# Decay attention and an MLP on one core: v's load in two column halves, with the splits and the next maximum at other heads

## The chip, the cores and the metric

The kernel runs on one core of one Trainium2 chip. The metric is the device time of one execution in microseconds; lower is better. Beside the times there is one profiled execution, whose span (first to last instruction) is a little shorter than the time that is measured from outside.

## The reference

There are 8 batches of 8 heads, 576 rows and 64 columns a head. Attention comes first, then an MLP over all 4608 rows of 512 columns, with 2048 columns in its middle:

```python
scores = scale * np.matmul(q, k.transpose(0, 1, 3, 2))
log_f = np.log(np.clip(f, 0.0001, 1.0))
cum = np.cumsum(log_f, axis=-1)
scores = np.where(causal, -1000000000.0, scores + cum[:, :, :, None] - cum[:, :, None, :])
attn = np.exp(scores - np.max(scores, axis=-1, keepdims=True))
attn = attn / (np.sum(attn, axis=-1, keepdims=True) + 1e-09)
x = np.matmul(attn, v)              # then (B*S, H*D)
h = x @ w_in
g = h * np.clip(h + 3.0, 0.0, 6.0) / 6.0
return g @ w_out
```

## The kernel before

Every large product runs on TensorE (PE) in fp16, with each operand split into a high and a low part, and three matmuls for one product (high by high, high by low, low by high). To split v, the kernel first needs a power-of-two scale for each batch, and for that the largest absolute value of the batch's v.

The main loop goes over 68 units: four "A" units and eight "B" units for batch 0, which is cut differently, and 56 "F" units, one for each head of batches 1 to 7. The names in the listings carry the unit's number: unit 12 is head 0 of batch 1, unit 20 head 0 of batch 2, and so on, so unit 36 is head 0 of batch 4 and unit 40 is head 4 of batch 4. One F unit does this:

- SP loads q and k of the head into one of three buffers ST (L411), decay rows into TK and TQ (L417, L419), and copies the rounded parts within the chip into T7 and T1 (L453, L454, both called T in the profile). POOL rounds q and k (L446, L447) and makes the rests (L455, L458).
- PE makes the scores pn (L608, L611) in two halves of the head's rows, called pn_40_0 and pn_40_1 for unit 40. DVE adds the mask and takes row maxima (L619), and makes the bias nb (L625). ACT takes the exponential (L631) and casts it into a ring buffer (L645). DVE or POOL puts the rest beside it (L648, L654, L659).
- SP transposes the ring buffer into pT by DMA (L666), once for each half.
- PE multiplies pT with the split v into pav (L691 to L696). DVE divides by the row sums (L720 to L726). For every pair of heads, the result is split (xhl, L731, L732) and transposed by DMA into xT (L752).

Between the pieces of this, the MLP is filled in, in nine tiles of 512 rows. Its first product (L778 to L780) makes ph; ACT and DVE make r and the two parts of gT out of it (L788, L791, L792, L793). Its second product (L800 to L802) makes po from all of gT, which ACT scales and SP stores (L811, L812). With half a unit or so of shift, one batch of attention goes with one tile of the MLP, so the first product, the second product, and the next first product lie in turn beside the heads of a batch.

For v there is one buffer, vst, which holds a whole batch: 128 partitions, 5 chunks of rows, 8 heads of 65 columns (64 and one spare). The first 64 rows go into chunk 0 twice (L359, two DMAs); the rest, 4 chunks of 520 columns in fp32, comes in one DMA of 1040 KB (L360). `load_v` for the next batch stands at head 6 of a batch. `v_scale` for the next batch stands at head 7: two reductions on DVE, of three and of two chunks (L365), two small steps (L370, L371), a matmul with ones that spreads the maximum (L183), and four small steps that make the scale (L178 to L199). `v_split` makes the fp16 parts of one pair of heads in v16, which has three slots: two ACT and two DVE instructions (L396, L397). It stands at heads 1, 3 and 5 for pairs 1 to 3 of the batch, and at head 7 for pair 0 of the next batch.

The framework's scheduler sets the order of the instructions on each engine from this program. A statement's place gives it its rank; an instruction that is ready by the scheduler's reckoning may be put far ahead of its place. Each engine then takes its instructions strictly in that order, and so does SP with its DMAs. An instruction that waits therefore holds up all that stands behind it on its engine.

Of the kernel before, what the change touches and what calls it, by code (L numbers as in the profile page):

```python
# [15 lines left out]
ALU = mybir.AluOpType  # L16
AX = mybir.AxisListType
# [3 lines left out]
def kernel(  # L21
# [10 lines left out]
    nc = tc.nc  # L32

    NHEAD, D, S = qk.shape
# [72 lines left out]
    POOL_REST = ((0, 0, 0, 0), (0, 0, 0, 0))  # L107
    PIN_V = 1
    TQ = [cpool.tile([97, SP], F32R, name=f"TQ{i}") for i in range(NQK)]
    TK = [cpool.tile([97, SP], F32R, name=f"TK{i}") for i in range(NQK)]  # L110
# [31 lines left out]
    v0 = [t.rearrange("p (c e) -> p c e", e=VR) for t in v0]  # L142

    def v_parts(b):
        return v0 if b == 0 else [vst[:, 0:3], vst[:, 3:]]

    def v_chunk(b, c):
        return v_parts(b)[c // 3][:, c % 3]

# [198 lines left out]

    def load_v(b):
        src = vS[b]  # L350
        lo, hi = v_parts(b)
        with pinned() if PIN_V else nullcontext():
            if b == 0:
                nc.sync.dma_start(lo, src[0:3 * P].rearrange("(c p) e -> p c e", p=P))
                nc.sync.dma_start(hi[:, 0], src[3 * P:4 * P])
                nc.sync.dma_start(hi[:64, 1], src[4 * P:S])
            else:
                for p in (0, 64):
                    nc.sync.dma_start(vst[p:p + 64, 0], src[0:64])  # L359
                nc.sync.dma_start(vst[:, 1:], src[64:].rearrange("(c p) e -> p c e", p=P))  # L360

    def v_scale(b):
        pm = p2.tile([P, 2], F32, tag="pm", name=f"vm{b}")
        for i, t in enumerate(v_parts(b)):
            nc.vector.tensor_reduce(  # L365
                pm[:, i:i + 1], t.rearrange("p c (h e) -> p (c h) e", e=D + 1)[:, :, 0:D],
                axis=AX.XY, op=ALU.max, apply_absolute_value=True,
            )
            yield
# [554 lines left out]
    for i, (kind, n) in enumerate(VH):  # L924
# [7 lines left out]
        if ahead:  # L932
            load_c(i + 2)
        if b + 1 < B and h == 6:
            load_v(b + 1)
        if b and h % 2 == 1 and h < H - 1:
            v_split((n + 1) // 2)
        if moved is not None:
# [10 lines left out]
        fill(1)  # L949
        if b + 1 < B and h == 7:  # L950
            vq = v_scale(b + 1)
# [20 lines left out]
        fill(1)  # L972
        if b + 1 < B and h == 7:
            for _ in vq:
                pass
            if b:
                v_split((n + 1) // 2)
        for _ in range(wn - wn // 2):
# [59 lines left out]
```

## Time and profile before

| | |
|---|---|
| three runs | 1094.02, 1103.02, 1099.4 us |
| their median | 1099.4 us |
| span of the profiled execution | 1093.0 us |
| TensorE busy | 1013.8 us (93%) |
| VectorE, ScalarE, GpSimd busy | 728.9, 609.7 and 414.4 us |
| mean granted TensorE clock | 0.981 |
| data moved by DMA | 133.74 MB |

Only a span is known of the profiled execution; it is about 1 us under the fastest run. The table's busy times are sums over the whole span. How much of a stage TensorE uses, and who stops it there, has to be read from short stretches, from the waits, and from the chain of waits that ended last. In a row of the waits stand the total in microseconds, how many there were, and the longest. In a row of a timeline stand the start, the length, the engine, the line, the operation, the tile written and the tile read, and in square brackets the idle time ahead of it and what ended that. "SPq" marks the issue of a DMA on SP; its transfer goes on after it.

### The profile page before, as it was taken

Reading aid. Unit: us, or ns where it says so; the run is one execution under the profiler, and the core shown is the slowest. Engines: PE = TensorE matmul, PEld = TensorE weight load, DVE = VectorE, ACT = ScalarE, POOL = GpSimd, SP = SyncE. Lnnn points to the kernel's source line nnn. Section 1 sums busy time; section 2 is a strip of 40 time slices with the busy share of each in tenths; the row PEclk is TensorE's granted clock in tenths of the full one; section 3 lists DMA queues with packets and bytes.
Section 4 is the critical chain, followed back from the end, with each engine's and each line's share of the span. In section 5 each row is a group of like instructions: output and inputs, shape, how many; then the busy total and the mean of one; then the engine's idle time right before and its main releaser. Section 6 shows DMA issues by size and latency. Waiting matters only on the chain.

```text
span 1093.0 us, 20322 instructions
## 1 busy us (share of the span) xinstructions
PE 1013.8 (93%) x7074; PEld 576.3 (53%) x7074; DVE 728.9 (67%) x1903; ACT 609.7 (56%) x1285; POOL 414.4 (38%) x505
## 2 busy tenths in 40 slices
PE   2799977899999989998999889999999999999998
PEld 2568844755555545554555445555555554444443
DVE  7888889877887669756876588569856840520520
ACT  4786656756765557545754566458646831621520
POOL 8443465345545434444534335453555300000000
PEclk9999989999999989998999989999999999999999
DMA  8966447866767656566566755785566530000001
GB/s 251 283 196 211 119 101 131 182 139 137 169 136 155 144 138 130 108 145 155 108 121 129 170 105 116 146 185 104 116 136 145 98 77 29 1 5 34 1 1 39
DMA packets 261651, 133.74 MB, mean 122 GB/s; under 512 B 229445, under 2 KB 231037, under 8 KB 261549
## 3 DMA queue, kind: packets, MB, share of 16 engines
q1 hardware_dynamic: 261548, 132.45, 54.0%
q8 instruction: 56, 0.92, 0.4%
q14 instruction: 47, 0.38, 0.1%
HBM read 47.93 MB, written 9.73 MB: 53 GB/s over the span
## 4 chain that ended last, share of the span: by engine, by line
PE 59%; DMA 6%; DVE 4%; issue 3%; SPq 3%; ACT 3%; POOL 2%; POOLq 0%; DVEq 0%; ACTq 0%
PE po L800 9%; PE po L802 9%; PE po L801 9%; PE ph L778 8%; PE ph L779 8%; PE ph L780 8%; DMA pT<-ring 3%; PE pn L611 3%; PE pn L608 3%; DMA vst<-in_vS_dram 2%; SPq L752 2%; DVE pp L619 1%; ACT pp L631 1%; PE pav L695 1%; PE pav L696 1%
## 5 line engine op out<-in xcount | busy, mean ns | idle before, releaser
L778 PE MATMUL ph<-xT,w 128*128 128x512 f16 (+1 forms) x640 | 229.2, 364 | 19.6 <-DVE r L791 19.4
L779 PE MATMUL ph<-xT,w 128*128 128x512 f16 (+1 forms) x640 | 228.5, 363 | 0.0
L780 PE MATMUL ph<-xT,w 128*128 128x512 f16 (+1 forms) x640 | 228.2, 362 | 0.0
L801 PE MATMUL po<-w,gT 128*128 128x512 f16 x576 | 214.3, 381 | 7.3 <-DVE w L294 7.3
L800 PE MATMUL po<-w,gT 128*128 128x512 f16 x576 | 212.1, 381 | 3.0 <-ACT w L283 2.2
L802 PE MATMUL po<-w,gT 128*128 128x512 f16 x576 | 214.1, 381 | 0.0
L631 ACT ACTIVATE pp<-pp,nb 128x192 f32<-128x192 f32 x280 | 138.8, 553 | 128.2 <-DVE nb L625 127.9
L648 DVE TENSOR_TENSOR ring<-pp,ring 128x128 f16<-128x128 f32 (+2 forms) x216 | 135.0, 635 | 70.1 <-ACT ring L645 69.2
L791 DVE SCALAR_TENSOR_TENSOR r<-r,ph 128x512 f32<-128x512 f32 (+1 forms) x160 | 99.9, 626 | 104.6 <-ACT r L788 104.4
L788 ACT ACTIVATE r<-ph,bias_r,SC 128x256 f32<-128x256 f32 (+7 forms) x272 | 144.1, 571 | 37.2 <-PE ph L780 33.3
L458 POOL TENSOR_TENSOR T<-ST,T 64x576 fp32r<-64x576 f32 (+1 forms) x68 | 100.6, 1480 | 153.5 <-DMA T<-TK 149.6
L792 ACT CAST gT<-r 128x512 f16<-128x512 f32 (+1 forms) x160 | 91.9, 575 | 89.6 <-DVE r L791 89.5
L619 DVE CUSTOM_DVE_ANT_0 pp<-pn,W 128x192 f32<-128x192 f32 x280 | 123.3, 482 | 26.1 <-PE pn L611 19.8
L608 PE MATMUL pn<-TK,TQ 68*128 68x192 f32 x336 | 127.0, 390 | 5.6 <-issue 4.0
L793 DVE TENSOR_TENSOR gT<-r,gT 128x512 f16<-128x512 f32 (+1 forms) x160 | 110.4, 693 | 29.2 <-ACT gT L792 28.5
L611 PE MATMUL pn<-T,T 128*128 128x192 f32 x336 | 116.2, 375 | 0.4 <-POOL T L458 0.4
L645 ACT CAST ring<-pp 128x192 f16<-128x192 f32 x280 | 115.7, 452 | 0.0
L455 POOL TENSOR_TENSOR T<-ST,TQ 64x576 fp32r<-64x576 f32 (+2 forms) x68 | 96.8, 1423 | 18.4 <-PE pn L611 8.7
L779 PEld LDWEIGHTS <-w 128*128 128x128 f16 x640 | 63.1, 99 | 75.2 <-issue 26.2
L780 PEld LDWEIGHTS <-w 128*128 128x128 f16 x640 | 63.2, 99 | 65.8 <-issue 9.2
L802 PEld LDWEIGHTS <-gT 128*128 128x128 f16 x576 | 56.5, 98 | 76.0 <-issue 14.6
L778 PEld LDWEIGHTS <-w 128*128 128x128 f16 x640 | 62.4, 99 | 59.1 <-issue 10.8
(136 smaller groups left out, 1713.6 us busy)
## 6 DMA issues: line engine op xcount, KB each, us to landing
ST<-in_qk_dram SPq DMA_DIRECT2D x64, 288.0 KB
T<-TK SPq DMA_DIRECT2D x64, 144.0 KB
out_dram<-o SPq DMA_DIRECT2D x36, 256.0 KB
ring<-in_w_out_dram SPq DMA_DIRECT2D x16, 512.0 KB
T<-TQ SPq DMA_DIRECT2D x56, 144.0 KB
vst<-in_vS_dram SPq DMA_DIRECT2D x7, 1040.0 KB
ring<-in_w_in_dram SPq DMA_DIRECT2D x9, 512.0 KB
w<-in_w_in_dram SPq DMA_DIRECT2D x7, 512.0 KB
```

The source lines that it names most:

```text
L608: nc.tensor.matmul(dst, TQ[i][0:D + 4, qs], TK[i][0:D + 4, a:e], start=True, stop=False)
L611: nc.tensor.matmul(dst, T7[j][:, qs], T1[j][:, a:e], start=False, stop=True)
L619: nc.vector.tensor_tensor_reduce(pp[:r, w:w + kw], pn[:r, o:o + kw], W[:r, 4 * P + r - kw:4 * P + r], 1.0, -3.0e38, ALU.add, ALU.max, accu ...
L631: nc.scalar.activation(x_, x_, AF.Exp, bias=nb[:r, e0 + x:e0 + x + 1], scale=0.125)
L648: eng.tensor_tensor(hl[:r, a:a + c * P], pp[:r, at[c] + 64:at[c] + kw], hl[:r, h0[c] + 64:h0[c] + kw], op=ALU.subtract,)
L778: nc.tensor.matmul(ph, w1[0][:, cc, fs_], xh, start=(cc == 0), stop=False)
L779: nc.tensor.matmul(ph, w1[0][:, cc, fs_], xl, start=False, stop=False)
L780: nc.tensor.matmul(ph, w1[1][:, cc, fs_], xh, start=False, stop=(cc == NCC - 1))
L788: nc.scalar.activation(r[:, a:e], ph[:, a:e], AF.Relu, bias=bias_r, scale=scol(A1 + NG * b + fc * NG // NFC))
L800: nc.tensor.matmul(po, gT[:, 0, fc, ts_], w2[:, fc, 0, :], start=(fc == 0), stop=False)
L801: nc.tensor.matmul(po, gT[:, 0, fc, ts_], w2[:, fc, 1, :], start=False, stop=False)
L802: nc.tensor.matmul(po, gT[:, 1, fc, ts_], w2[:, fc, 0, :], start=False, stop=(fc == NFC - 1))
```

## The change

The buffer vst stays one buffer, but a batch now comes in two halves of 260 columns, heads 0 to 3 and heads 4 to 7, each with its own three DMAs. The halves are loaded at heads 2 and 4 of the batch before. Pairs 1, 2 and 3 of a batch are split at heads 1, 2 and 3. The two reductions go over one half each, all five chunks, and stand at head 6. The split of the next batch's pair 0 stays at head 7.

```diff
+    V_LOAD, V_SPLIT, V_MAX = (2, 4), (1, 2, 3), 6
...
+    def v_cols(half):
+        return slice(half * (VR // 2), (half + 1) * (VR // 2))
+
     def v_parts(b):
-        return v0 if b == 0 else [vst[:, 0:3], vst[:, 3:]]
+        return v0 if b == 0 else [vst[:, :, v_cols(half)] for half in range(2)]
...
-    def load_v(b):
+    def load_v(b, half=None):
...
+                cols = v_cols(half)
                 for p in (0, 64):
-                    nc.sync.dma_start(vst[p:p + 64, 0], src[0:64])
-                nc.sync.dma_start(vst[:, 1:], src[64:].rearrange("(c p) e -> p c e", p=P))
+                    nc.sync.dma_start(vst[p:p + 64, 0, cols], src[0:64, cols])
+                nc.sync.dma_start(
+                    vst[:, 1:, cols], src[64:, cols].rearrange("(c p) e -> p c e", p=P)
+                )
...
-                pm[:, i:i + 1], t.rearrange("p c (h e) -> p (c h) e", e=D + 1)[:, :, 0:D],
-                axis=AX.XY, op=ALU.max, apply_absolute_value=True,
+                pm[:, i:i + 1], t.rearrange("p c (h e) -> p c h e", e=D + 1)[:, :, :, 0:D],
+                axis=AX.XYZ, op=ALU.max, apply_absolute_value=True,
...
-        if b + 1 < B and h == 6:
-            load_v(b + 1)
-        if b and h % 2 == 1 and h < H - 1:
-            v_split((n + 1) // 2)
+        if b + 1 < B and h in V_LOAD:
+            load_v(b + 1, V_LOAD.index(h))
+        if b and h in V_SPLIT:
+            v_split(NPAIR * b + 1 + V_SPLIT.index(h))
...
-        if b + 1 < B and h == 7:
+        if b + 1 < B and h == V_MAX:
             vq = v_scale(b + 1)
...
-        if b + 1 < B and h == 7:
+        if b + 1 < B and h == V_MAX:
             for _ in vq:
                 pass
-            if b:
-                v_split((n + 1) // 2)
+        if b and b + 1 < B and h == H - 1:
+            v_split(NPAIR * (b + 1))
```

The line numbers move by 5 to 7: L359, L360, L365, L411, L453, L619, L648, L666 and L752 of the kernel before are L364, L365, L372, L418, L460, L626, L655, L673 and L759 of the changed one.

Three places of the order bear on what follows, all for the v of batch 5, which is loaded during batch 4. The first is on VectorE, around unit 40, where the kernel before takes the maximum vm5 (ISA rows on pp and MF are the mask with the row maxima; r and gT belong to the MLP). Before:

```order
L619 ISA pp_40_0_6132,MF0_108<-pn_40_0_6123,W_88 64x64
L619 ISA MF0_108 64x1
L791 SCALAR_TENSOR_TENSOR r_3_3_0_6112<-r_3_3_0_6112,ph_3_3_0_6053 128x512
L625 TENSOR_SCALAR nb_40_6122<-MF0_108 128x3
L793 TENSOR_TENSOR gT_116<-r_3_3_0_6112,gT_116 128x512
L619 ISA pp_40_1_6187,MF0_108<-pn_40_1_6182,W_88 128x320
L619 ISA MF0_108 128x1
L619 ISA pp_40_1_6187,MF0_108<-pn_40_1_6182,W_88 128x448
L619 ISA MF0_108 128x1
L365 TENSOR_REDUCE vm5_6689<-vst_112 128x1 x2
```

Now:

```order
L800 TENSOR_TENSOR gT_116<-r_3_2_0_6066,gT_116 128x512
L372 TENSOR_REDUCE vm5_6527<-vst_112 128x1
L626 ISA pp_40_0_6154,MF0_108<-pn_40_0_6145,W_88 128x192
L626 ISA MF0_108 128x1
L626 ISA pp_40_0_6154,MF0_108<-pn_40_0_6145,W_88 128x576
L626 ISA MF0_108 128x1
```

Both reductions stood behind the second half of unit 40; one of them now stands ahead of its first half, and behind the gT of the r ahead.

The second is on SP, at the load that this maximum reads (pT_39 are the transposes of unit 39). Before:

```order
L666 DMA_TRANSPOSE pT_39_5939<-ring0_123 128x13x128
L419 DMA TQ0_93<-decay_dram 2x576
L453 DMA T71_102<-TQ2_95 64x576
L454 DMA T11_100<-TK2_98 64x576
L666 DMA_TRANSPOSE pT_39_5939<-ring1_124 128x12x128
L360 DMA vst_112<-in_vS_dram 128x4x520
```

Now, with the half that holds heads 4 to 7:

```order
L673 DMA_TRANSPOSE pT_39_5958<-ring0_123 128x13x128
L426 DMA TQ0_93<-decay_dram 2x576
L365 DMA vst_112<-in_vS_dram 128x4x260
L460 DMA T71_102<-TQ2_95 64x576
L673 DMA_TRANSPOSE pT_39_5958<-ring1_124 128x12x128
L461 DMA T11_100<-TK2_98 64x576
```

The load has moved from behind the second transpose of unit 39 to a place ahead of it, behind the first.

The third is on SP again, some four units earlier, where the half with heads 0 to 3 goes in (T, ST and TQ are the buffers of a coming unit; xT are the MLP's inputs). Before:

```order
L752 DMA_TRANSPOSE xT1_118<-xhl_32_5088 128x4x64
L666 DMA_TRANSPOSE pT_35_5276<-ring2_125 128x12x128
L453 DMA T71_102<-TQ1_94 64x576
L454 DMA T11_100<-TK1_97 64x576
L411 DMA ST1_104<-in_qk_dram 128x576
L812 DMA out_0_dram<-o_2_0_5492 128x512
L417 DMA TK0_96<-decay_dram 2x576
L419 DMA TQ0_93<-decay_dram 2x576
```

Now:

```order
L460 DMA T71_102<-TQ1_94 64x576
L461 DMA T11_100<-TK1_97 64x576
L418 DMA ST1_104<-in_qk_dram 128x576
L364 DMA vst_112<-in_vS_dram 64x260 x2
L759 DMA_TRANSPOSE xT0_117<-xhl_32_5103 128x2x64
L673 DMA_TRANSPOSE pT_35_5300<-ring1_124 128x13x128
L759 DMA_TRANSPOSE xT0_117<-xhl_32_5103 128x4x64
L759 DMA_TRANSPOSE xT1_118<-xhl_32_5103 128x4x64
L759 DMA_TRANSPOSE xT0_117<-xhl_32_5103 128x4x64
L759 DMA_TRANSPOSE xT1_118<-xhl_32_5103 128x4x64
L673 DMA_TRANSPOSE pT_35_5300<-ring2_125 128x12x128
L365 DMA vst_112<-in_vS_dram 128x4x260
```

The two T copies and the ST load stood behind the transposes of unit 35 and now stand ahead of them, together with two small pieces of v; the half itself follows the last transpose. Its reduction is on VectorE, at a place that held none. Before:

```order
L619 ISA pp_36_1_5522,MF0_108<-pn_36_1_5517,W_88 128x448
L619 ISA MF0_108 128x1
L648 TENSOR_TENSOR ring0_123<-pp_36_0_5472,ring0_123 128x512
L625 TENSOR_SCALAR nb_36_5462<-MF0_108 128x2
L648 TENSOR_TENSOR ring1_124<-pp_36_1_5522,ring1_124 128x256
L648 TENSOR_TENSOR ring1_124<-pp_36_1_5522,ring1_124 128x384
```

Now:

```order
L626 ISA pp_36_1_5534,MF0_108<-pn_36_1_5529,W_88 128x448
L626 ISA MF0_108 128x1
L655 TENSOR_TENSOR ring0_123<-pp_36_0_5484,ring0_123 128x512
L372 TENSOR_REDUCE vm5_6527<-vst_112 128x1
L632 TENSOR_SCALAR nb_36_5474<-MF0_108 128x2
L655 TENSOR_TENSOR ring1_124<-pp_36_1_5534,ring1_124 128x256
L655 TENSOR_TENSOR ring1_124<-pp_36_1_5534,ring1_124 128x384
```

The reduction of the first half stands between the row maxima of unit 36 and the bias nb_36 that is made from them.

More of the change, by code (lines that the diff above doesn't have):

```diff
@@ L142 @@
     v0 = [t.rearrange("p (c e) -> p c e", e=VR) for t in v0]
+    def v_cols(half):
+        return slice(half * (VR // 2), (half + 1) * (VR // 2))
     def v_parts(b):
-        return v0 if b == 0 else [vst[:, 0:3], vst[:, 3:]]
+        return v0 if b == 0 else [vst[:, :, v_cols(half)] for half in range(2)]
     def v_chunk(b, c):
-        return v_parts(b)[c // 3][:, c % 3]
+        return v0[c // 3][:, c % 3]
     NG = 4
@@ L346, in w_out_work @@
             yield
-    def load_v(b):
+    def load_v(b, half=None):
         src = vS[b]
-        lo, hi = v_parts(b)
+        lo, hi = v_parts(0)
         with pinned() if PIN_V else nullcontext():
```

## Prediction

> **What bounds the kernel now.** I read the page first, then the waits, the chain of waits, and TensorE's share by stretch.
>
> ```profile
> PE 1013.8 (93%) x7074; PEld 576.3 (53%) x7074; DVE 728.9 (67%) x1903; ACT 609.7 (56%) x1285; POOL 414.4 (38%) x505
> ```
>
> TensorE works in 93% of a span of 1093.0 us, so 79 us of idle PE are all that any change of order can win. The waits (us in total, times, longest) say which part of that belongs to v:
>
> ```profile
> DVE vm L365 <- DMA vst<-in_vS_dram: 26.7, 6, 9.3
> ...
> PE ph L778 <- DVE r L791: 19.4, 6, 7.8
> ```
>
> VectorE (DVE) waited six times, 26.7 us together, for v to land before it could take the maximum. TensorE's largest wait in the MLP's first product names r, which DVE makes, also six times. The chain of waits has the load in it (start, length):
>
> ```profile
> 392.56 6.15 DMA vst<-in_vS_dram
> ```
>
> This load of 1040 KB takes 6.15 us from issue to landing. The two reductions follow it, and behind them on DVE the r that L778 waits for. These five of the six waits matter below (start, length of both reductions, idle time ahead of them):
>
> ```profile
> 219.38 2.88 DVE L365 TENSOR_REDUCE vm<-vst 128x1 f32<-128x1536 f32 x2 [1.35 <-DMA vst<-in_vS_dram]
> ...
> 398.73 2.88 DVE L365 TENSOR_REDUCE vm<-vst 128x1 f32<-128x1536 f32 x2 [6.25 <-DMA vst<-in_vS_dram]
> ...
> 512.55 2.88 DVE L365 TENSOR_REDUCE vm<-vst 128x1 f32<-128x1536 f32 x2 [6.09 <-DMA vst<-in_vS_dram]
> ...
> 628.31 2.88 DVE L365 TENSOR_REDUCE vm<-vst 128x1 f32<-128x1536 f32 x2 [9.32 <-DMA vst<-in_vS_dram]
> ...
> 735.24 2.88 DVE L365 TENSOR_REDUCE vm<-vst 128x1 f32<-128x1536 f32 x2 [2.65 <-DMA vst<-in_vS_dram]
> ```
>
> TensorE over short stretches (length, PE busy, then the other engines, granted clock, DMA share, GB/s):
>
> ```profile
> 215.00:235.00 20.00, 18.00 (x147) 12.65 (x146) 16.87 (x48) 12.18 (x29) 7.36 (x9) 0.91 0.69 158
> 392.00:402.00 10.00, 5.08 (x58) 2.95 (x57) 3.75 (x5) 2.02 (x6) 5.69 (x7) 0.94 0.78 215
> 402.00:408.00 6.00, 5.74 (x19) 3.27 (x19) 5.88 (x20) 5.02 (x10) 0.70 (x2) 0.54 0.64 123
> 440.00:475.00 35.00, 35.00 (x281) 19.85 (x280) 22.97 (x66) 16.75 (x36) 14.12 (x19) 1.00 0.61 117
> 505.00:515.00 10.00, 6.05 (x63) 3.36 (x62) 3.49 (x6) 2.99 (x8) 4.83 (x7) 0.92 0.90 220
> 515.00:520.00 5.00, 3.92 (x13) 2.43 (x13) 4.97 (x14) 3.94 (x9) 1.39 (x1) 0.50 0.45 104
> 623.00:632.00 9.00, 1.86 (x39) 1.41 (x38) 3.69 (x4) 0.00 (x0) 6.19 (x7) 0.86 0.72 210
> 632.00:637.00 5.00, 4.38 (x17) 2.69 (x17) 5.00 (x14) 4.37 (x9) 0.60 (x1) 0.57 0.66 144
> 725.00:745.00 20.00, 20.00 (x170) 11.62 (x168) 16.62 (x39) 13.37 (x30) 7.77 (x11) 1.00 0.75 164
> ```
>
> The loads for batches 4, 5 and 6 stop TensorE: it is idle for 4.92 + 0.26 = 5.2 us, 3.95 + 1.08 = 5.0 us and 7.14 + 0.62 = 7.8 us, 18.0 us in all. The granted clock then stays near half speed: 0.54 x 6, 0.50 x 5 and 0.57 x 5 us cost about 2.6, 2.0 and 1.9 us of full-speed work, 6.5 us. DVE was held (wait plus reductions) for 9.1, 9.0 and 12.2 us at these places, so TensorE rode out the first 4 us each time; around 735 us DVE was held 5.5 us, and TensorE has 20.00 of 20 us. A hold of up to 4 or 5.5 us is free. The stretch at 215 to 235 us lost another 2.0 us plus 0.09 x 20 = 1.8 us at a wait of 1.35 us, partly for other reasons. The stretch from 440 to 475, in the second product, has no idle TensorE at all.
>
> **The change at the old place.** A half is 520 KB and comes in 128x4x260 plus two small pieces. No transfer of that size from HBM at this load stands in the rows, so I bound it: half of 6.15, 3.1 us, from below, and 6.15, no gain, from above. A smaller transfer is in the trace:
>
> ```profile
> 450.02 0.59 SPq L454 DMA_DIRECT2D T<-TK  x1
> ...
> 452.71 1.43 POOL L458 TENSOR_TENSOR T<-ST,T 64x576 fp32r<-64x576 f32 x1 [5.52 <-DMA T<-TK]
> ```
>
> 144 KB was used 2.7 us after issue. A line through 144 KB in 2.7 and 1040 KB in 6.15 gives 4.1 us for 520 KB; I take that. The reductions each go over five chunks and half the columns, 1280 elements, between the two forms of now:
>
> ```profile
> L365 DVE TENSOR_REDUCE vm<-vst x14: 1208/1481/1754, 120.5 to 736.9; 128x1 f32<-128x1536 f32 x7, 128x1 f32<-128x1024 f32 x7
> ```
>
> 1754 ns for 1536 and 1208 for 1024 give 1.48 us for 1280. The sum of both stays 2.96 us, but only one of them now stands at the old place. If the first half is done, the hold there should shrink by 2 us of landing and 1.5 us of reduction.
>
> The order takes most of the first saving back. The second half's load goes out before the second transpose of pT_39 rather than after it, but its reduction has moved too, ahead of pp_40_0 instead of behind pp_40_1. Where DVE and SP stood then, in the times of before:
>
> ```profile
> 501.42 0.36 DVE L619 CUSTOM_DVE_ANT_0 pp<-pn,W 128x192 f32<-128x192 f32 x1
> ```
>
> ```profile
> 502.10 0.78 SPq L419 DMA_DIRECT2D TQ<-decay_dram  x1
> ...
> 505.78 1.13 SPq L360 DMA_DIRECT2D vst<-in_vS_dram  x1
> ```
>
> For batch 5 the reduction is reached at 501.4 and the load issued at 502.9 (502.10 + 0.78), so it lands at 507.0: a wait of 5.6 where it was 6.09. With 1.48 us of work the hold is 7.1 us, 1.9 less than 9.0. The same rows for batches 4 and 6:
>
> ```profile
> 387.44 0.36 DVE L619 CUSTOM_DVE_ANT_0 pp<-pn,W 128x192 f32<-128x192 f32 x1
> ...
> 388.71 0.96 SPq L419 DMA_DIRECT2D TQ<-decay_dram  x1
> ...
> 615.73 0.67 DVE L791 SCALAR_TENSOR_TENSOR r<-r,ph 128x512 f32<-128x512 f32 x1
> ...
> 619.49 1.29 SPq L666 DMA_TRANSPOSE pT<-ring  x1
> ```
>
> Batch 4: reached 387.4, issued 389.7, landed 393.8; hold 6.4 + 1.5 = 7.9, 1.2 less. Batch 6: reached 616.4, issued 620.8, landed 624.9; hold 8.5 + 1.5 = 10.0, 2.2 less. At these three places every microsecond of hold is one of TensorE, so the gain is 1.2 + 1.9 + 2.2 = **5.3 us**. For batch 2 both halves go out long before they are read; of the 3.8 us lost there I credit **3 us**, since only part of it follows the wait. Batches 3 and 7 are at or under the free hold: nothing.
>
> **The new place.** The other half adds a load and a reduction per batch in the middle of the attention of a batch, where DVE waited for nothing before. Behind that reduction stand nb_36, the subtraction into ring1 and with them pT_36. For batch 5 the rows are:
>
> ```profile
> 437.32 1.14 POOL L447 TENSOR_SCALAR TQ<-ST 64x576 fp32r<-64x576 f32 x1
> ...
> 437.96 4.86 SPq L752 DMA_TRANSPOSE xT<-xhl  x3
> ...
> 447.51 1.44 SPq L666 DMA_TRANSPOSE pT<-ring  x1
> ...
> 452.20 0.69 DVE L648 TENSOR_TENSOR ring<-pp,ring 128x512 f16<-128x512 f32 x1
> ...
> 462.91 1.42 SPq L666 DMA_TRANSPOSE pT<-ring  x1
> ...
> 468.68 0.19 PE L691 MATMUL pav<-v,pT 128*128 128x65 f16 x1
> ```
>
> In the new order two T copies, the ST load that waits for POOL, and two pieces of v stand ahead of seven transposes that ran from 437.96 to 448.95. The copies can go once POOL has written TQ, at 438.5; they land 2.7 us later, POOL subtracts for 1.43, and the ST load goes at about 443.5. The transposes begin near 445, 7 us late; the last ends at 455.8, and the half behind it lands at 459.9. DVE reaches its reduction at 452.9: a wait of 7.0 and a hold of 8.5 us. For batches 3 and 4:
>
> ```profile
> 248.08 0.48 DVE L726 TENSOR_TENSOR xf<-pav,rs 128x320 f32<-128x320 f32 x1
> ...
> 250.43 0.36 SPq L411 DMA_DIRECT2D ST<-in_qk_dram  x1
> ...
> 342.86 1.06 DVE L625 TENSOR_SCALAR nb<-MF 128x2 f32<-128x2 f32 x1
> ...
> 343.58 0.47 SPq L453 DMA_DIRECT2D T<-TQ  x1
> ```
>
> Batch 3: reached 248.6, the load behind the blocked ST load, about 251, landed 255: hold 6.5 + 1.5 = 8.0. Batch 4: reached 343.9, issued about 344.4 (two pieces and the rest where the second T copy stood), landed 348.5: hold 6.1. For batches 6 and 7 the same working gives 4 us, within the free hold; batches 1 and 2 wait for nothing.
>
> What does such a hold cost TensorE here? From below: nothing, if the second product goes on, for its matmuls read neither r nor a new gT. From above: the same 4 us of cover as in the first product, 4.5 + 4.0 + 2.1 = 10.6 us, plus a low clock of 2 us after two of them, 14.6 us. The rows lie between: ring1 comes about 8.5 us late, pT_36's second half was issued at 462.91 behind POOL, which gives back 4 of these, and pav_36 began at 468.68, some 4 us after that transpose ended; TensorE runs in order, so the attention product would stop it for 1 or 2 us. I take **5 us** for all batches.
>
> **The rest.** Each batch has three more DMAs on SP, 21 more in all; the second half now stands ahead of a pT transpose and holds it back by 1.1 us, the length of the L360 issue, and pT_35 comes late, which I count as one more of that size. From below 0, from above 8 x 1.1 = 8.8 us; since TensorE waits for pT only at some heads, **2.5 us**. The earlier splits for pairs 1 to 3 are the same instructions on ACT and DVE, at 56% and 67% busy; they cost nothing while those have room, and 0.55 us each otherwise. The scheduler gave much of the order before 220 us another shape; I put 0 there, with 5 us either way.
>
> Sum: -5.3 - 3 + 5 + 2.5 = **-0.8 us** on the span of 1093.0. The profiled execution is in line with the fastest of the three runs, 1094.0; the median, 1099.4, is 0.5% above. I forecast **1098.6 us** for the median: no change that a measurement of this kernel could tell, which is about 1%, 11 us.
>
> One rule bears on the low clock. The rows for batch 5, of one microsecond each:
>
> ```profile
> 511.00:512.00 1.00, 0.05 (x2) 0.00 (x0) 0.00 (x0) 0.00 (x0) 0.43 (x2) 1.00 1.05 390
> ...
> 513.00:514.00 1.00, 0.00 (x0) 0.00 (x0) 1.00 (x1) 0.00 (x0) 0.00 (x0) 0.69 0.78 165
> ```
>
> TensorE stops at the start of the first; in the second the mean clock is 0.69, so it fell about 2.4 us after the stop. The Trainium skill, TensorE: Matmul & The Clock Gate, section Part 1: The HAM clock gate, says that the array falls to half its clock after an idle window of about 3.4 us, on a window that runs free. By that rule the stops for batches 4 and 5, 4.0 and 3.1 us after the change, would at times keep their clock, and the sum would be up to 4 us lower; by the row of 2.4 us they would not, and my sum leaves them.
>
> **The rivals.** *The halves land in time.* If SP reaches the loads earlier than in my working, all waits fall under the free hold: 18.0 idle, 6.5 of clock and 3 at batch 2 go, 27.5 us, so 1072. For it: the load needs only 4 of the 6 us. Against it: its place on SP is bound to pT and to the v splits, and DVE's place has moved up as far.
>
> *The new waits are covered.* If the second product hides them and SP's extra issues, only the gain is left: 5.3 + 3 and up to 4 of clock, so 1087 to 1091. For it: no idle TensorE from 440 to 475 although pT is on SP's queue there. Against it: pav stands in order with the second product.
>
> *The new waits stop TensorE.* The half load is behind an SP queue that POOL blocks, DVE is held 6 to 8.5 us, nb, ring and pT come late, and pav stops TensorE at up to three more places, with half the clock behind two of them. That is 14.6 + 8.8 against 5.3 + 3, so +15: 1114. It decides from the point at which the hold costs more than it wins, a cost of about 20 us for a slower kernel by 1%; a fourth stop of the size of those now, 5 + 2 us, would do it.
>
> *Both halves late together.* If the column halves count as one buffer for the order, the first half's load waits for the last split; then nothing is early and the time stays, with 1.5 us of SP time per batch: 1100 to 1108. The order listing, which puts the first half's reduction half a batch ahead, speaks against it.
>
> **How the numbers follow.** Forecast 0.47, with its own range 1089 to 1108; halves in time 0.13; new waits covered 0.15; new waits stop TensorE 0.19; both late 0.06. The covered case is over 1% faster about half of the time, and the unknown order leaves 0.03 of the forecast beyond each bound. Faster: 0.13 + 0.07 + 0.03 = 0.23; slower: 0.18 + 0.03 + 0.01 = 0.22; within 1%: 0.55. The range goes from 1079, which leaves most of the first rival out, to 1115, which leaves half of the third.
>
> **What would show it.** Right: vm waits near 450 and 250 us of 5 us or more with TensorE going on; at the old places waits of 5.5 to 8.5 us, one reduction of 1.48 us behind each, and TensorE stopping for 4, 3 and 5.5 us. The reductions' wait in total would rise from 26.7 to about 40 us while the span stays. Wrong: old waits under 3 us and no stretch at half clock (first rival), or idle TensorE behind L691 and L696 near 255, 350 and 465 us (third). An issue-to-landing time of the halves far from 4.1 us would break the sum first.

## The result and the profile after

The changed kernel takes 1109.51 us (median of four runs, 1108.57 to 1110.71) against 1098.19 us for the kernel before: a ratio of 1.0107, 95% interval 1.0078 to 1.0136. It is slower by 1.1%, some 12 us, where the forecast was 0.8 us faster and no change that one could tell. The span and the engines' busy time on the page after:

```profile
span 1107.1 us, 20329 instructions
...
PE 1019.1 (92%) x7074; PEld 578.9 (52%) x7074; DVE 729.4 (66%) x1903; ACT 609.1 (55%) x1285; POOL 410.4 (37%) x505
```

The span grew by 14.1 us, more than the medians did, because the profiled execution of the kernel before was the fastest of its four. TensorE (PE) was idle for 1107.1 - 1019.1 = 88.0 us instead of 79.2, and its busy time grew by 5.3 us, part of which is matmuls at a low clock. The waits (total, times, longest):

```profile
DVE vm L372 <- DMA vst<-in_vS_dram: 41.1, 8, 8.5
...
PE ph L785 <- DVE r L798: 27.6, 8, 6.0
...
DVE vm L372 <- issue: 13.9, 2, 10.1
```

The waits for v on VectorE (DVE) went from 26.7 us in six to 41.1 in eight. Two more, 13.9 us, stand under "issue"; they end at the same reductions. TensorE's wait for r grew from 19.4 to 27.6 us. Here are the reductions one by one, for batches 3 to 7 (start, length, the tile, and the idle time ahead in brackets; the second half's of batch 3, with a wait of 4.77 us, and the first half's of batch 7, with 0.02, are left out):

```profile
253.21 1.49 DVE L372 TENSOR_REDUCE vm<-vst 128x1 f32<-128x1280 f32 x1 [3.88 <-issue]
...
350.08 1.49 DVE L372 TENSOR_REDUCE vm<-vst 128x1 f32<-128x1280 f32 x1 [4.37 <-DMA vst<-in_vS_dram]
...
401.90 1.49 DVE L372 TENSOR_REDUCE vm<-vst 128x1 f32<-128x1280 f32 x1 [10.06 <-issue]
...
467.58 1.49 DVE L372 TENSOR_REDUCE vm<-vst 128x1 f32<-128x1280 f32 x1 [6.38 <-DMA vst<-in_vS_dram]
...
518.91 1.49 DVE L372 TENSOR_REDUCE vm<-vst 128x1 f32<-128x1280 f32 x1 [8.50 <-DMA vst<-in_vS_dram]
...
571.02 1.49 DVE L372 TENSOR_REDUCE vm<-vst 128x1 f32<-128x1280 f32 x1 [0.85 <-DMA vst<-in_vS_dram]
...
635.23 1.49 DVE L372 TENSOR_REDUCE vm<-vst 128x1 f32<-128x1280 f32 x1 [7.80 <-DMA vst<-in_vS_dram]
...
744.29 1.49 DVE L372 TENSOR_REDUCE vm<-vst 128x1 f32<-128x1280 f32 x1 [7.37 <-DMA vst<-in_vS_dram]
```

The rows at 253, 350, 468 and 571 us are those of the first half, at the new place. The rows at 402, 519, 635 and 744 us are those of the second half, at the old place. The reduction takes 1.49 us, as reckoned. But the waits at the old place, 10.1, 8.5, 7.8 and 7.4 us, are longer than those of before for three of the four batches (6.25, 6.09, 9.32 and 2.65 in the kernel before). TensorE around them (length, PE busy, PEld, DVE, ACT, POOL, granted clock, DMA share, GB/s):

```profile
345.00:360.00 15.00, 15.00 (x115) 8.25 (x114) 8.43 (x24) 6.13 (x13) 9.78 (x12) 1.00 0.87 170
397.00:411.00 14.00, 6.23 (x53) 3.05 (x54) 9.10 (x21) 5.55 (x13) 6.32 (x8) 0.63 0.65 148
460.00:470.00 10.00, 8.79 (x80) 5.13 (x79) 2.75 (x5) 0.98 (x4) 3.05 (x4) 1.00 0.87 182
515.00:526.00 11.00, 4.53 (x19) 1.66 (x18) 7.09 (x18) 3.50 (x9) 4.43 (x5) 0.69 0.67 156
634.00:646.00 12.00, 6.56 (x47) 3.96 (x44) 10.33 (x21) 7.38 (x17) 7.98 (x8) 0.72 0.53 122
742.00:751.00 9.00, 4.74 (x16) 2.07 (x15) 6.71 (x18) 2.23 (x5) 3.52 (x5) 0.81 0.87 206
```

At the old place TensorE is idle for 7.8, 6.5, 5.4 and 4.3 us, 23.9 in all where it was 18.0 in the kernel before, and batch 7, which had cost nothing, is now among them. The granted clock there is 0.63 to 0.81. At the new place TensorE loses nothing (345 to 360 us) or 1.2 us (460 to 470 us), although VectorE waited 4.4 and 6.4 us there.

Why the second half is late is in the rows for batch 5. VectorE came to the reduction at 510.4, the end of this row:

```profile
509.72 0.68 DVE L800 TENSOR_TENSOR gT<-r,gT 128x512 f16<-128x512 f32 x1
```

SP at that time:

```profile
505.18 6.34 SPq L759 DMA_TRANSPOSE xT<-xhl  x5
511.62 0.38 SPq L424 DMA_DIRECT2D TK<-decay_dram  x1
512.12 1.47 SPq L673 DMA_TRANSPOSE pT<-ring  x1
513.64 0.78 SPq L426 DMA_DIRECT2D TQ<-decay_dram  x1
514.47 0.41 SPq L365 DMA_DIRECT2D vst<-in_vS_dram  x1
```

SP was still issuing the five xT transposes then. Behind them stood a decay load, the first pT transpose and another decay load; the half went out at 514.47, 4.1 us after VectorE had begun to wait for it, and was used 4.4 us later.

### The profile page after: what moved, and what is told of

Read it like the earlier page. It is cut to its first block, busy times and chain, and to the rows that moved or that the text cites. A ratio compares the mean times of both kernels' runs of the same rounds, so it can differ in the third digit from the quotient of the medians.

```text
span 1107.1 us, 20329 instructions
## 1 busy us (share of the span) xinstructions
PE 1019.1 (92%) x7074; PEld 578.9 (52%) x7074; DVE 729.4 (66%) x1903; ACT 609.1 (55%) x1285; POOL 410.4 (37%) x505
## 4 chain that ended last, share of the span: by engine, by line
PE 66%; DVE 13%; issue 6%; DMA 6%; ACT 5%; POOL 2%; SPq 2%; DVEq 0%; ACTq 0%; POOLq 0%
PE po L807 10%; PE po L808 10%; PE po L809 10%; PE ph L785 8%; PE ph L786 8%; PE ph L787 8%; DVE pp L626 3%; PE pn L618 3%; PE pn L615 2%; DVE ring L655 2%; DMA vst<-in_vS_dram 2%; ACT pp L638 2%; DMA pT<-ring 2%; DVE gT L800 2%; PE pav L709 2%
## 5 line engine op out<-in xcount | busy, mean ns | idle before, releaser
L785 PE MATMUL ph<-xT,w 128*128 128x512 f16 (+1 forms) x640 | 231.8, 367 | 30.8 <-DVE r L798 27.6
L655 DVE TENSOR_TENSOR ring<-pp,ring 128x128 f16<-128x128 f32 (+2 forms) x216 | 137.8, 651 | 65.5 <-ACT ring L652 64.5
L800 DVE TENSOR_TENSOR gT<-r,gT 128x512 f16<-128x512 f32 (+1 forms) x160 | 116.0, 727 | 27.4 <-ACT gT L799 26.9
L626 DVE CUSTOM_DVE_ANT_0 pp<-pn,W 128x192 f32<-128x192 f32 x280 | 122.7, 481 | 13.6 <-PE pn L618 11.9
L787 PEld LDWEIGHTS <-w 128*128 128x128 f16 x640 | 63.7, 100 | 65.9 <-issue 10.1
```

What stands on the lines that cost most here:

```text
L626: nc.vector.tensor_tensor_reduce(pp[:r, w:w + kw], pn[:r, o:o + kw], W[:r, 4 * P + r - kw:4 * P + r], 1.0, -3.0e38, ALU.add, ALU.max, accu ...
L655: eng.tensor_tensor(hl[:r, a:a + c * P], pp[:r, at[c] + 64:at[c] + kw], hl[:r, h0[c] + 64:h0[c] + kw], op=ALU.subtract,)
L785: nc.tensor.matmul(ph, w1[0][:, cc, fs_], xh, start=(cc == 0), stop=False)
L787: nc.tensor.matmul(ph, w1[1][:, cc, fs_], xh, start=False, stop=(cc == NCC - 1))
```

## The experiments

Three theories stood at the beginning. **A**: what stops TensorE is VectorE's hold (wait plus reduction) at the second half's reduction. **B**: time is lost in SP's queue, to late T and pT, and the waits for v only show it. The third was the rival of the prediction by which the new place of the first half stops TensorE. **A1** to **A4**, below, are ways in which the hold of A could have come about.

To take a wait away, a reduction was tied behind the row maxima of a later unit on VectorE, by when v has landed. For batches 2 to 7:

```diff
+    def LATE(b, i):
+        return (NPAIR + H * (b - 1) + (1, 5)[i], 1)
...
+            with tc.issue_after(mark[LATE(b, i)].ins) if b > 1 else nullcontext():
                 nc.vector.tensor_reduce(
...
-                nc.vector.tensor_tensor_reduce(
+                mark[v, half] = nc.vector.tensor_tensor_reduce(
```

Here `mark` keeps the row maxima (L619 of before, in `rows`) of each unit, i = 0 is the first half and i = 1 the second, and the unit is that of head 1 or head 5. The tie names VectorE alone, but the scheduler then set the order of the other engines anew, so SP's order did not stay as it is in the change, as the texts below expected. With the first half alone tied it nearly did: from 340 us on, the rows differ from the change's only in the place of the tied reductions and in five pT transposes on SP. With the second half tied, the orders differ from 185 us on, TensorE's too. Each of these runs thus tests the tie together with what the scheduler made of it.

**The second half's reduction later** (the diff above, with `b > 1 and i == 1`):

> The change, with the reduction of the second half (heads 4 to 7) alone tied behind the row maxima of a later unit (head 5, second half) in VectorE's order, for batches 2 to 7; SP's order stays as it is in the change. Theory A (the hold of VectorE at the second half's reduction is what stops TensorE, about 24 us idle and 8 us of low clock in the profile of the change): the four stops near 400, 520, 640 and 745 us go, 24 to 32 us less than the change, so 1078 to 1086 us. Theory B (the time goes to the halves' place on SP and to late T and pT, and the waits only show it): the stops move to other waits, 1100 to 1109 us.

Measured: 1090.0 us, ratio to before 0.9947 (0.9926 to 0.9968), 1.6% under the change. That is some 18 us of the 24 to 32 expected. Around the places of the second half the long stops went; in the stretch from 380 to 900 us of each kernel TensorE was busy as follows, first in the change, then here:

```profile
380.00:900.00 520.00, 492.83 (x3643) 269.90 (x3642) 378.67 (x964) 312.16 (x676) 229.29 (x287) 0.97 0.61 128
```

```profile
380.00:900.00 520.00, 500.97 (x3763) 275.05 (x3762) 375.16 (x962) 308.38 (x667) 222.23 (x281) 1.00 0.63 128
```

Idle time there fell from 27.2 to 19.0 us, and the clock's mean rose from 0.97 to 1.00. TensorE's waits in that stretch (total, times, longest) say where the idle time went, first in the change, then here:

```profile
PE ph L785 <- DVE r L798: 21.4, 4, 6.0
PE pav L698 <- DMA pT<-ring: 3.8, 3, 1.8
```

```profile
PE pav L703 <- DMA pT<-ring: 11.3, 8, 3.9
PE ph L790 <- DVE r L803: 4.0, 4, 1.2
```

The waits for r, which stand behind the hold, all but went, as A says. The waits for pT, which comes through SP's queue, grew from 3.8 to 11.3 us: that part came back elsewhere in short stops, as B would have it.

**The first half's reduction later** (`b > 1 and i == 0`):

> The change, with the reduction of the first half (heads 0 to 3) alone tied behind the row maxima of a later unit (head 1, second half), for batches 2 to 7. Theory A: the new place costs TensorE little, 1 to 5 us less than the change, so 1104 to 1109 us, and the four stops at the second half stay. The third rival of the prediction (the new waits stop TensorE): 10 to 15 us less, 1095 to 1100 us.

Measured: 1102.26 us, ratio 1.0056 (1.0028 to 1.0083), 0.5% or 5.6 us under the change, with some 4 us either way. The third rival's 10 to 15 us are out. The four waits of the second half stayed:

```profile
395.36 1.49 DVE L377 TENSOR_REDUCE vm<-vst 128x1 f32<-128x1280 f32 x1 [10.23 <-issue]
...
510.26 1.49 DVE L377 TENSOR_REDUCE vm<-vst 128x1 f32<-128x1280 f32 x1 [6.99 <-DMA vst<-in_vS_dram]
...
627.46 1.49 DVE L377 TENSOR_REDUCE vm<-vst 128x1 f32<-128x1280 f32 x1 [8.00 <-DMA vst<-in_vS_dram]
...
736.14 1.49 DVE L377 TENSOR_REDUCE vm<-vst 128x1 f32<-128x1280 f32 x1 [6.60 <-DMA vst<-in_vS_dram]
```

10.2, 7.0, 8.0 and 6.6 us, so the first half's hold is not what makes the second half late; at most it adds 1.5 us for batch 5 and less for the others. Nor is the gain to be found at the new places of batches 4 to 7: in the profiled executions this run is 8 us ahead of the change at 344 us (in the times of before), where the orders of the engines still differ, and 7 us at the end.

**Both later** (the diff above):

> The change, with both reductions tied to the later units. Theory A: as with the second half alone, and 1 to 5 us less, 1074 to 1084 us; no wait for v on VectorE over 1 us from batch 3 on. Theory B: 1095 to 1108 us with the same idle time on TensorE at other waits.

Measured: 1085.73 us, ratio 0.9910 (0.9882 to 0.9938). The two gains add up within their intervals, 17.6 and 5.6 us against 21.6 us together. No wait for v is left from batch 3 on. The time is 2 us above what A expected, 4 us by the ratio, and idle time from 380 to 900 us is 15.6 us:

```profile
380.00:900.00 520.00, 504.42 (x3745) 275.63 (x3745) 371.05 (x953) 305.55 (x661) 220.02 (x277) 1.00 0.62 127
```

**The kernel before, with its reductions later** (the same tie, both behind head 5):

> The kernel before, whole batches in one load, with both of its reductions tied behind the row maxima of the unit at head 5, second half, for batches 2 to 7. Theory A: its three stops (18.0 us idle, 6.5 us of low clock) go, 1071 to 1080 us, so the halves are not needed to lose the wait. Theory B: the wait turns up elsewhere, 1090 to 1099 us.

Measured: 1083.4 us, ratio 0.9877 (0.9856 to 0.9899): 13.5 us less than before, though not the 18 to 27 that A expected. The same stretch of the kernel before, and of this one:

```profile
380.00:900.00 520.00, 500.67 (x3753) 276.03 (x3751) 375.39 (x965) 310.19 (x670) 224.22 (x281) 0.98 0.62 128
```

```profile
380.00:900.00 520.00, 511.86 (x3824) 280.39 (x3823) 381.91 (x978) 314.33 (x678) 224.19 (x285) 1.00 0.63 130
```

19.3 us of idle time became 8.1. At the old places TensorE gained 16.7 us by the rows of its attention product pav; it was 5.2 us late ahead of 384 us, where the order had changed as well. So the wait can be lost without halves, and the whole load is at least as fast as the halves with both ties, within their intervals.

**The second half's reduction back at the old place** (`LATE` gives head 4, second half, for i = 1 alone): 5 us later than in the change, with the change's loads.

> The change, with the second half's reduction tied behind the row maxima of the unit at head 4, second half: the place that the whole batch's reductions had in the kernel before, some 5 us later than in the change; SP's order is the change's. Theory A1 (the hold grew because the reduction moved further ahead than its load did): DVE waits 3 to 5 us there for batches 4, 5 and 6, holds of 4.5 to 6.5 us against a free hold of 4 to 5.5, and the time falls by 10 to 16 us from the change, to 1094 to 1100 us at a before of 1098 (ratio 0.996 to 1.002). Theory A2 (the load itself lands later than a whole batch's did): waits of 7 us or more stay, ratio 1.006 to 1.010.

Measured: 1103.04 us, ratio 1.0065 (1.0045 to 1.0086). The waits:

```profile
401.60 1.49 DVE L377 TENSOR_REDUCE vm<-vst 128x1 f32<-128x1280 f32 x1 [4.59 <-issue]
...
515.10 1.49 DVE L377 TENSOR_REDUCE vm<-vst 128x1 f32<-128x1280 f32 x1 [1.12 <-DMA vst<-in_vS_dram]
...
631.30 1.49 DVE L377 TENSOR_REDUCE vm<-vst 128x1 f32<-128x1280 f32 x1 [5.83 <-DMA vst<-in_vS_dram]
...
739.84 1.49 DVE L377 TENSOR_REDUCE vm<-vst 128x1 f32<-128x1280 f32 x1 [0.80 <-DMA vst<-in_vS_dram]
```

For batches 4 to 6 A1 expected 3 to 5 us; 4.6, 1.1 and 5.8 came, all under A2's 7 us, and 0.8 for batch 7. With 1.5 us of reduction these are holds of 6.1, 2.6, 7.3 and 2.3 us, all under those of the kernel before. But the time fell by only 0.4%, 4.6 us, and not by 10 to 16. Idle time from 380 to 900 us fell from 27.2 to 20.4 us. TensorE's waits in that stretch show why it did not fall further:

```profile
PE pav L703 <- DMA pT<-ring: 14.8, 12, 2.5
PE ph L790 <- DVE r L803: 5.1, 3, 3.7
```

The waits for r fell from 21.4 to 5.1 us, and the waits for pT rose from 3.8 to 14.8. The table has the same by stage. It goes by the start of the same pav matmul in each run: the first row says how much later than in the kernel before TensorE comes to it at 384 us, the others how much it falls back in a stage, or catches up (minus). Stages are named by where they lie in the kernel before.

| TensorE falls back (us) | the change | second half later | first half later | second half at the old place |
|---|---|---|---|---|
| ahead of 384 us | 3.7 | -1.7 | -3.7 | 4.5 |
| 384 to 428, old place, batch 4 | 2.4 | -2.3 | 3.3 | -2.2 |
| 428 to 482, new place, batch 5 | 2.0 | 6.2 | 1.7 | 5.0 |
| 482 to 541, old place, batch 5 | 1.3 | -4.8 | 0.5 | -3.8 |
| 541 to 595, new place, batch 6 | 1.2 | 1.8 | 0.4 | 2.8 |
| 595 to 657, old place, batch 6 | -2.4 | -6.1 | -2.7 | -3.5 |
| 657 to 711, new place, batch 7 | 0.9 | 1.3 | 1.4 | 0.4 |
| 711 to 884, old place, batch 7, and the rest | 4.8 | 1.3 | 6.0 | 3.7 |
| in all | 13.9 | -4.3 | 6.9 | 6.9 |

At the old places the last column is 11.8 us better than the change, which is what A1 expected of the time. Of that, 4.0 us are lost again in the stages between, where TensorE now waits for pT on SP, and 0.8 us ahead of 384 us. So A1 has the hold right, and B fits what the time lost again; TensorE's order changed with this tie too, so the two are not fully apart.

**The loads written one head sooner**, each behind the split that frees its half:

```diff
-    V_LOAD, V_SPLIT, V_MAX = (2, 4), (1, 2, 3), 6
+    V_LOAD, V_SPLIT, V_MAX = (1, 3), (1, 2, 3), 6
...
-        if b + 1 < B and h in V_LOAD:
-            load_v(b + 1, V_LOAD.index(h))
         if b and h in V_SPLIT:
             v_split(NPAIR * b + 1 + V_SPLIT.index(h))
+        if b + 1 < B and h in V_LOAD:
+            load_v(b + 1, V_LOAD.index(h))
```

> The change, with both loads written one head sooner, just behind the split that frees their half (heads 1 and 3 in place of 2 and 4). On SP the second half's load now goes ahead of the five xT transposes; on VectorE its reduction has also moved up by about a unit. Theory A1 (the order puts the reduction where the scheduler takes the load to have landed, ahead of the real landing, wherever the load stands): waits of 5 to 9 us as in the change, ratio to before 1.006 to 1.014. Theory A3 (the wait is the xT transposes ahead of the load): waits under 3 us, ratio 0.985 to 0.997.

Measured: 1113.55 us, ratio 1.0161 (1.0123 to 1.0200), the slowest of all. The second half's waits:

```profile
397.26 1.49 DVE L372 TENSOR_REDUCE vm<-vst 128x1 f32<-128x1280 f32 x1 [9.37 <-DMA vst<-in_vS_dram]
...
517.00 1.49 DVE L372 TENSOR_REDUCE vm<-vst 128x1 f32<-128x1280 f32 x1 [8.86 <-DMA vst<-in_vS_dram]
...
632.47 1.49 DVE L372 TENSOR_REDUCE vm<-vst 128x1 f32<-128x1280 f32 x1 [6.39 <-DMA vst<-in_vS_dram]
...
745.31 1.49 DVE L372 TENSOR_REDUCE vm<-vst 128x1 f32<-128x1280 f32 x1 [7.97 <-DMA vst<-in_vS_dram]
```

9.4, 8.9, 6.4 and 8.0 us, although the load now went ahead of the xT transposes. A3, by which these transposes are the wait, is out. The reduction had moved up with the load, as A1 says: an earlier load alone wins nothing here.

**The loads from ScalarE's queue** (`nc.scalar.dma_start` in place of `nc.sync.dma_start` for batches 1 to 7, in the change). The reductions come to stand where they stand with the loads written sooner, so the two can be laid side by side:

> The change, with the loads of v for batches 1 to 7 issued from ScalarE's queue in place of SP's; nothing else. Their second half goes out ahead of the exponential of the unit at head 3, its reduction stands behind the first row maxima of that unit, which is the same place on VectorE as with the loads written sooner (waits there of 9.4, 8.9, 6.4 and 8.0 us). Theory A4 (SP's queue, full of transposes and later than VectorE, is what the load waits in): issue by ScalarE comes 1 us or so ahead of VectorE's arrival, waits of 2 to 5 us, ratio to before 0.990 to 1.000. Rival A1 alone (the reduction is as far ahead of any load): waits of 6 to 9 us, ratio 1.005 to 1.016.

Measured: 1089.75 us, ratio 0.9955 (0.9928 to 0.9982), 1.5% under the change. The second half's waits:

```profile
393.64 1.49 DVE L372 TENSOR_REDUCE vm<-vst 128x1 f32<-128x1280 f32 x1 [2.10 <-DMA vst<-in_vS_dram]
...
503.71 1.49 DVE L372 TENSOR_REDUCE vm<-vst 128x1 f32<-128x1280 f32 x1 [1.44 <-DMA vst<-in_vS_dram]
...
612.99 1.49 DVE L372 TENSOR_REDUCE vm<-vst 128x1 f32<-128x1280 f32 x1 [1.24 <-DMA vst<-in_vS_dram]
...
719.48 1.49 DVE L372 TENSOR_REDUCE vm<-vst 128x1 f32<-128x1280 f32 x1 [0.81 <-DMA vst<-in_vS_dram]
```

2.1, 1.4, 1.2 and 0.8 us where they were 9.4, 8.9, 6.4 and 8.0. From 380 to 900 us TensorE is idle for 8.5 us:

```profile
380.00:900.00 520.00, 511.53 (x3864) 281.52 (x3861) 380.73 (x983) 314.98 (x682) 230.68 (x292) 1.00 0.63 133
```

These waits are at the lower end of A4's 2 to 5 us or under it. For batch 5 ScalarE issued the half at 498.05, 4.2 us before VectorE came to the reduction; with the loads written sooner SP issued it at 512.29, 4.2 us after. The wait therefore needs both: a reduction placed close to where its load goes out, and a load that SP issues late. The order of the other engines moved as well in this run, so it shows what the queue is worth only together with that.

**ScalarE's queue with both reductions later**, in the change:

> The change with both reductions tied to the later units (heads 1 and 5), and the loads issued from ScalarE's queue in place of SP's. From 380 to 900 us, idle time and low clock of TensorE together are 17.3 us with the tie alone, 9.8 in the kernel before with its tie. Theory A4 (what is left of the halves' price is their three more DMAs per batch on SP, which pT and xT stand behind): 5 to 10 us in that stretch, ratio to before 0.982 to 0.989. Rival (the halves cost by themselves, by two places on VectorE): 14 us or more there, ratio 0.990 or more.

Measured: 1081.23 us, ratio 0.9849 (0.9813 to 0.9885), where both ties alone gave 0.9910. Idle time from 380 to 900 us is 9.0 us instead of 15.6:

```profile
380.00:900.00 520.00, 511.03 (x3818) 280.18 (x3817) 377.57 (x969) 312.16 (x675) 223.75 (x282) 1.00 0.62 129
```

Together with 1.7 us of low clock that is 10.7 us, slightly over the 5 to 10 expected and under the rival's 14. So most of the idle time that the halves still had with both ties went with their loads off SP. The orders of all engines differ between the two runs from the start, and the intervals of the ratios touch, so it is not shown that the issues alone did it.

**ScalarE's queue in the kernel before, with its reductions later** (whole loads):

> The kernel before with its reductions tied behind the unit at head 5, and its whole loads issued from ScalarE's queue in place of SP's. The three issues per batch leave SP, whose transposes TensorE waits for, and take ScalarE's time instead (about 2 us a batch). Theory A4: a little faster than with the tie alone (0.9877), 0.982 to 0.987. Rival: ScalarE's issues hold up the exponentials, 0.989 or more.

Measured: 1080.65 us, ratio 0.9872 (0.9843 to 0.9900), the same as with the tie alone. Taking the three issues per batch off SP was worth nothing that can be measured here; the expected small gain is not there.

**One part alone: the splits at heads 1, 2 and 3**, in the kernel before, with whole loads:

```diff
-        if b and h % 2 == 1 and h < H - 1:
-            v_split((n + 1) // 2)
+        if b and h in (1, 2, 3):
+            v_split(NPAIR * b + h)
...
             if b:
-                v_split((n + 1) // 2)
+                v_split(NPAIR * (b + 1))
```

The last two lines write the split of the next batch's pair 0, which stays where it was, in the new counting.

> The kernel before with one part of the change alone: pairs 1, 2 and 3 split at heads 1, 2 and 3 in place of 1, 3 and 5; whole loads, whole reductions at their old places. The order stays nearly that of before around the loads. Theory A: no part of the loss, ratio 0.997 to 1.003. Rival (earlier splits hold ACT up behind pav): 1.004 or more.

Measured: 1097.16 us, ratio 1.0013 (0.9987 to 1.0040). The earlier splits cost nothing by themselves that can be measured here.

**The halves alone**, with the old splits (`V_LOAD, V_SPLIT, V_MAX = (2, 6), (1, 3, 5), 7`):

> The change's column halves with the splits at heads 1, 3 and 5, the loads at heads 2 and 6 and the maximum at head 7, as far as the old splits allow it. The second half's load goes behind the second pT transpose again, its reduction behind the first half of the unit at head 4. Theory A: two holds per batch all the same, the second about 7 to 8 us by the times of before (9 for a whole batch), ratio 1.000 to 1.010. Rival (the loss comes from the earlier places of load, splits and maximum, not from the halves): 0.993 or less.

Measured: 1102.38 us, ratio 1.0048 (1.0026 to 1.0071). About half of the loss is there with the halves alone. The waits at the second half are 9.7, 8.2, 8.1 and 5.4 us; with 1.5 us of reduction the holds for batches 4 to 6 are 11.2, 9.7 and 9.6 us, where 7 to 8 were expected.

**A later place still for the kernel before** (`LATE` gives head 6):

> The kernel before with its reductions tied behind the unit at head 6, second half, one unit further than the run with head 5. Theory A: once no wait is left, a later place gives nothing more, 0.985 to 0.990, the same as 0.9877. Rival (the place itself matters, since the scale is needed for the next batch's first splits): 0.992 or more.

Measured: 1078.24 us, ratio 0.9838 (0.9810 to 0.9866), a shade under the expected 0.985 to 0.990; its interval overlaps that of the tie to head 5. From 380 to 900 us TensorE is idle for 4.6 us:

```profile
380.00:900.00 520.00, 515.42 (x3847) 282.52 (x3846) 384.19 (x977) 314.71 (x679) 225.34 (x283) 1.00 0.64 131
```

This is the lowest ratio of all, though its interval overlaps those of the three other runs around 0.985. The kernel before with a tie on the order of its reductions beats both kernels, by 1.6% and, through before, by 2.7%.

## Why the prediction was wrong, point by point

**The second half's term, -5.3 us, had the wrong sign; this is the step that failed.** It worked out where VectorE would reach the reduction and when SP would issue the load, and took both in the times of before, as if the two fell behind by the same amount. Both did come at the places in the order that it names. But for batch 5 SP's decay load ahead of the half was issued at 513.64 where it was 502.10, 11.5 us later, while VectorE's row ahead of the reduction began at 509.72 where it was 500.59, 9.1 us later. So the half went out 4.1 us after VectorE's arrival, not 1.5. The same two rows are 7.7 and 4.5 us late for batch 4 and, by the same working, 14.7 and 9.1 us for batch 7, for which the prediction worked nothing out; only for batch 6, by the rows that the prediction took there, is SP less late, 9.3 against 11.0 us. The waits follow this: 10.1 us for 6.4 that were predicted (batch 4), 8.5 for 5.6 (batch 5), 7.8 for 8.5 (batch 6), 7.4 for none (batch 7). TensorE's idle time at these places rose by 5.9 us, and by the table above it fell back there by 6.1 us, where a gain of 5.3 was forecast. These 11 us are most of what the sum is off.

**Where SP's delay came from.** The prediction had half of it in hand: at the new place it moved the transposes 7 us back, behind two T copies and an ST load that waits for POOL. But it did not carry SP's delay on to the second half's load. These are SP's rows at the new place of batch 5; in the kernel before, the xT transposes there began at 437.96:

```profile
446.83 0.59 SPq L461 DMA_DIRECT2D T<-TK  x1
451.17 0.37 SPq L418 DMA_DIRECT2D ST<-in_qk_dram  x1
451.63 1.13 SPq L364 DMA_DIRECT2D vst<-in_vS_dram  x2
452.86 1.20 SPq L759 DMA_TRANSPOSE xT<-xhl  x1
```

SP waited 3.8 us at the ST load, with the transposes behind it. They began 14.9 us later than before, where TensorE was 6.7 us late (its pav at 454.18 came at 460.89). How many us late the two were ahead of each second half, SP by the first of its xT transposes there, TensorE by a pav row within 6 us of that:

| batch | the change: TensorE | SP | first half's reduction later: TensorE | SP |
|---|---|---|---|---|
| 4 | 3.7 | 7.0 | -3.7 | 0.3 |
| 5 | 8.1 | 11.5 | 1.4 | 2.7 |
| 6 | 10.6 | 10.0 | 2.2 | 2.1 |
| 7 | 9.1 | 14.1 | 0.9 | 6.2 |

SP is 3.3, 3.5 and 5.0 us later than TensorE for batches 4, 5 and 7, and not for batch 6, where the wait came as reckoned. With the first half's hold gone it is still 4.0, 1.3 and 5.2 us later. So for batches 4 and 7 the delay is SP's own; it begins at the new place and stays up to the load. For batch 5 the hold makes 2 of the 3.5 us, and SP catches up once in between. The run with the halves alone says that the order makes more of it than the number of DMAs: it has the same added DMAs, but at the new place of batch 5 its T copies stand behind the transposes again (they go out at 455.95, the transposes from 444.25), and SP is only 1.6, 0.5, 1.8 and 1.9 us later than TensorE for batches 4 to 7. Other places of the order differ in that run too, so how much falls to the copies and how much to the ST load stays open. Its waits are long all the same: for batch 5 the half went out at 510.98, behind the second transpose as in the kernel before, and VectorE was there at 508.45.

**The sizes in that term held.** The half took 4.1 to 5.0 us from issue to use (4.1 predicted, for instance 345.94 to 350.08 and 630.23 to 635.23), and the reduction 1.49 us (1.48).

**The new place cost about what was put down, but not by the hold.** Waits of 7.0, 6.5 and 4.6 us were worked out for batches 5, 3 and 4; 6.4, 3.9 and 4.4 came. In the table of stages TensorE falls back by 4.1 us at the new places of batches 5 to 7, against a price of 5 us for all batches. But with the first half's reduction later it still falls back by 3.5 us there, so only 0.6 us of this goes with the hold that the prediction priced. What that run gained, 5.6 us in time, lies ahead of 344 us, where it changed more than the hold. That the price fits is in part luck.

**The rest was too low.** 2.5 us were taken for the added DMAs on SP, between 0 and 8.8. Between the halves and the whole load, with no waits for v in either from batch 3 on, lie 0.3% in time, 3.6 us, with intervals that overlap, and 7.5 us of idle TensorE from 380 to 900 us; with the loads off SP the halves come to 9.0 us, next to the 8.1 of the whole load on SP. This points to the upper part of the range; the times alone do not decide it.

**The 3 us for batch 2** can't be told from the new order ahead of 230 us.

**The rivals.** The third, slower by the new waits, had the right sign and nearly the right time, 1114 us, for a reason that fell: TensorE hardly stopped at the new waits, and its stops grew at the old place. The rival named a fourth stop as what would decide; one came, at the old place of batch 7. The range, 1079 to 1115, held the time.

**The signs that were named.** The wait for v was to rise from 26.7 to about 40 us while the span stays; it came to 55.0 us (41.1 + 13.9), and the span grew. TensorE going on at the new place, and a single reduction of 1.48 us behind each wait, came as said; stops of 4, 3 and 5.5 us at the old place came as 7.8, 6.5 and 5.4.

**The rule on the clock** (the Trainium skill, TensorE: Matmul & The Clock Gate, Part 1: The HAM clock gate) had 4 us to gain if the stops became shorter. Three of the four are over 5 us and all of them have a low clock behind them, so these runs neither bear the gain out nor speak against it.

## What to carry to other kernels

In this kernel the scheduler put the reduction ahead of where its load really landed, wherever the load stood: a smaller or an earlier load drew the reduction forward with it, and the wait stayed. Where you see this, put the consumer later by an explicit order, if its result isn't needed soon: here that took 1.2 to 1.6% off the kernel before, with its loads and splits as they were. Look at the next queue before you count the gain: with the hold made shorter in the change, TensorE waited for the transposes on SP instead, up to 14.8 us from 380 to 900 us.

And when a step is judged by who arrives first, the two must not both be read off the old trace. A queue in which a DMA that waits has moved ahead of others can be late at the next place too: SP was 2.4 to 5.7 us later than VectorE at three of the four loads, and the forecast gain became a loss.

## What was not expected of the hardware

SP only issues DMAs in this kernel, but its queue set the time of the load: for batch 5 the issues of five xT transposes took 6.34 us of it and that of one pT transpose 1.47, and the 520 KB behind them started only then. Loads of the same size from ScalarE's queue were waited for 0.8 to 2.1 us at the same place on VectorE, where those from SP's were waited for 6.4 to 9.4; the order of the other engines differed between these two runs.
